# Head dimensions in neighbouring pairs, copies for q and k first, banks handed back early, and pauses in a planned Trainium2 kernel

## The chip, the cores and the metric

The kernel runs on one core of a Trainium2 chip. The metric is the device time of one execution in microseconds. Engines are called as in the profile: PE (TensorE), DVE (VectorE), ACT (ScalarE), POOL (GpSimd) and SP (SyncE, which issues the DMAs).

## The reference

One attention layer (A) and one gated layer (B) share their weights between two rounds, so that four layers follow each other over 2048 positions of 576 numbers in bf16:

```python
x = x + A(layernorm(x)); x = x + B(layernorm(x))
x = x + A(layernorm(x)); x = x + B(layernorm(x))

# A: 32 heads of 18 dimensions; position s sees s, s-2, ..., s-14
q, k, v = split(x @ wqkv)                     # wqkv [576, 3*576], columns (q|k|v, head, dim)
logits[h, s, w] = sum_d q[h, s, d] * k[h, s - 2w, d] * 18**-0.5     # w = 0..7, masked below 0
o[h, s, d] = sum_w softmax_w(logits)[h, s, w] * v[h, s - 2w, d]
A = o @ wo
# B: F = 4608
B = ((x @ w_gate) * (x @ w_up)) @ w_down
```

## The kernel before

The 2048 positions are cut into blocks of 256 (the first two, j=0 and j=1, have 128), and the two rounds of layers are interleaved: a block of round 1 runs when its inputs from round 0 are there, so 17 blocks j follow each other. For each block there is an attention part (layer norm, projection, logits, softmax, weighted sum, output product) and a gated part (gate and up products, h, down product). PE works on the gated part of one block while DVE and ACT work on the attention of the next.

**Order.** Nothing is left to a compiler's scheduler. Every operation is entered in a `Plan` with an engine, a cost in ns, a priority and a rank, and a list scheduler (`Plan.run`) walks through clocks that it keeps per engine and issues the instructions in the order that results. An operation with `alts` may go to either of two engines, by their clocks. A raw weight piece has a planned landing time (`late`). PSUM banks are handed out as slots: a *unit* is a pair of banks `pg`, `pu` (slots 0 to 2), and `acct`, `pa` are a fourth pair, which becomes a unit (slot 3) after the attention of block 2. While PE would wait in the first block, the plan puts dummy matmuls into `acct` (`fill`, L1212).

**First block ("boot").** x and wqkv come by DMA in raw form, five pieces of 128 rows (the last of 64) of the q and k columns (a) and of the v columns (b). The copies of `perm` (L391 to L421) put the columns in the order (dim, head): 128x512 for the first 16 dims of q or k, 128x256 halves for v (L408), and small tails for dims 16 and 17 (128x128, 128x64). The projection (L609) needs, per piece, the copies of that piece. Then follow the evictions of q and k (L727, L720, L691), the products q*k (L764), the sum over dims by a matmul with the 0/1 matrix `Esel` (L779), the softmax (max L805, difference L809, exp L817, sum L821, reciprocal L826, L829, L830), the spread of the softmax weights over the dims by `Bsel` (L845), its eviction to `ab` (L850, shown as L691 on DVE and L693 on ACT), the products with v (L878), their sums on PE (L882, L883), wo (L943), the residual (L913), layer norm (L474, L476, L492, L493, L497, L508), transposes (L527, L529), `xnT_B` (L534), and the first gate product (L996).

**Later blocks.** Logits come from L787, L768, L772 and L773 on DVE, the weighted sum from L878 and L900 on DVE. From block 3 on, the softmax weights go out to `a_dram` (L855) and come back four times (L858), spread over partitions. wo is L922. The gated part is L996, L1007 and L1020 on PE, `g_sb` on ACT (L1031), h on DVE (L1035, L1038) and the down products (L1052, L1089, L1090). `tok` (L553) is a copy of one element on ACT that keeps an order between PE and another engine.

The line of the plan that decides when an operation may start takes an operation of the same engine at its end:

```python
for p in o.deps:
    e = p.ready if p.eng != o.eng else p.end
```

Of the kernel before, what the change touches and what calls it, by code (L numbers as in the profile page):

```python
# [11 lines left out]
ALU = mybir.AluOpType  # L12
# [4 lines left out]
class Op:  # L17
    __slots__ = ("eng", "cost", "fn", "deps", "order", "succ", "n", "prio", "idx", "hold", "free",
                 "lat", "margin", "ready", "end", "nbytes", "use", "pair", "need", "rank", "late", "half", "res", "alts", "risk")
# [4 lines left out]
VP = ["ACT"] * 5  # L24
VT = ["ACT"] * 5
# [8 lines left out]
class Plan:  # L34
# [13 lines left out]
    def op(self, eng, cost, fn, r=(), w=(), prio=1, after=None, hold=None, free=None, margin=0, nbytes=0, use=None,  # L48
           pair=None, need=None, due=False, late=0, half=False, alts=None, risk=0):
# [59 lines left out]
    def run(self, slots):  # L109
# [10 lines left out]
        while cand:  # L120
            best = None
            urgent = {}
            for o in cand:
# [87 lines left out]
def kernel(  # L211
# [43 lines left out]
    a_dram = [dram.tile([P, 2 * CH], BF16, name=f"a_dram{i}") for i in range(2)]  # L255
# [12 lines left out]
    Bsel = sb("Bsel", [P, 4, 4, 32])  # L268
# [93 lines left out]
    def load_w(c):  # L362
        wr, c0, c1 = ((wrawa, 0, 2 * D), (wrawb, 2 * D, 3 * D))[c == "b"]
        for k in range(KT):
            for r_, rows in ((0, P),) if k < KF else ((0, TL), (TL, TL)):
                def fn(k=k, r_=r_, rows=rows):
# [6 lines left out]
                   nbytes=rows * (c1 - c0) * 2, prio=1 + (c == "b"), late=700 if c == "a" else 0)  # L373
# [4 lines left out]
    def setup_b():  # L378
# [11 lines left out]
        for k in range(KT):  # L390
            def perm(eng, cost, key, t3, rk, k=k):  # L391
                if t3 < 3:
                    wr = wrawb[:, k, :] if t3 == 2 else wrawa[:, k, t3 * D:(t3 + 1) * D]
                    src = wr.rearrange("p (h d) -> p d h", h=H)[:, 0:16, :]
                    dst = wqkv[:, k, t3 * 512:(t3 + 1) * 512].rearrange("p (d h) -> p d h", h=H)
                else:
                    t0, t1 = (0, 2) if t3 == 3 else (2, 3)
                    src = (wrawa, wrawb)[t3 - 3][:, k, :].rearrange("p (t h d) -> p t d h", t=t1 - t0, h=H)[:, :, 16:18, :]
                    dst = wqkv[:, k, 3 * 512:3 * D].rearrange("p (t d h) -> p t d h", t=3, h=H)[:, t0:t1]
                fn = {"DVE": nc.vector.tensor_copy, "POOL": nc.gpsimd.tensor_copy, "ACT": nc.scalar.copy}[eng]  # L400
                pl.rank = 0.5
                if t3 == 2:
                    for hf in range(2):
                        box = {}

                        def half(hf=hf, box=box):
                            f = {"DVE": nc.vector.tensor_copy, "ACT": nc.scalar.copy}[box["o"].eng]
                            f(dst[:, 8 * hf:8 * hf + 8], src[:, 8 * hf:8 * hf + 8])  # L408
                        box["o"] = op("ACT", 565, half, r=rk, w=[f"{key}{'ab'[hf]}"], prio=3, alts={"DVE": 320, "ACT": 565})
                else:  # L410
                    op(eng, cost, lambda: fn(dst, src), r=rk, w=[key], prio=2 + (t3 == 4))  # L411
                pl.rank = 0
            ra, rb = [[f"wraw{c}{k}"] if k < KF else [f"wrawt{c}0", f"wrawt{c}{TL}"] for c in "ab"]
            perm("DVE", 530, f"wq0_{k}", 0, ra)
            perm("DVE", 180, f"wq3_{k}", 3, ra)
            if k % 2:
                perm("DVE", 530, f"wq1_{k}", 1, ra)
            else:
                perm("ACT", 1000, f"wq1_{k}", 1, ra)
            perm(VP[k], {"ACT": 1050, "DVE": 560, "POOL": 1250}[VP[k]], f"wq2_{k}", 2, rb)  # L420
            perm(VT[k], {"ACT": 330, "DVE": 200, "POOL": 300}[VT[k]], f"wq4_{k}", 4, rb)  # L421

        def mk_sel():
            nc.gpsimd.memset(Esel[:], 0.0)
            nc.gpsimd.memset(Bsel[:], 0.0)
            for j in range(4):
                nc.gpsimd.affine_select(out=Esel[:], in_=Esel[:], compare_op=ALU.not_equal,
                                        fill=1.0, base=-32 * j, pattern=[[-1, 32]], channel_multiplier=1)
                nc.gpsimd.affine_select(out=Bsel[:, j], in_=Bsel[:, j], compare_op=ALU.not_equal, fill=1.0,
                                        base=-32 * j, pattern=[[0, 4], [-1, 32]], channel_multiplier=1)  # L430
# [817 lines left out]
```

## Time and profile before

| | us |
|---|---|
| median of 3 runs | 1043.29 (1042.44 to 1043.44) |
| the profiled execution | 1042.26 |
| its span | 1040.1 |
| PE busy | 1029.8 (17905 matmuls) |
| DVE busy | 775.8 |
| ACT busy | 437.1 |
| POOL busy | 8.9 |

The span is what the profile covers, from the first to the last instruction; the profiled execution was 2.2 us longer than it. Busy times of different engines overlap. A line such as `PE pu L609 <- DVE wqkv L411: 0.4, 1, 0.4` says that PE's instruction of line 609 waited for DVE's of line 411: 0.4 us in all, once, 0.4 us at most.

### The profile page before, as it was taken

The numbers are of one execution on the slowest core, as the hardware profiler recorded it, in microseconds if no ns is written. First come the engines' busy times: TensorE is split into PE (matmuls) and PEld (weight loads), VectorE is DVE, ScalarE is ACT, GpSimd is POOL, SyncE is SP. The second block draws the span as 40 slices with busy tenths as digits, with TensorE's granted clock in tenths as the row PEclk, the third lists the DMA queues.
The fourth block names the chain that finished last, engine by engine and source line by source line (L and its number), as shares of the span: only waits on it lengthen the run. The fifth ranks groups of instructions, "written<-read, shape, count | busy, mean of one in ns | idle before, by whom it ended". The sixth has DMA issues, their size and how long they took to land.

```text
span 1040.1 us, 40101 instructions
## 1 busy us (share of the span) xinstructions
PE 1029.8 (99%) x17905; PEld 810.1 (78%) x17905; DVE 775.8 (75%) x1450; ACT 437.1 (42%) x1169; POOL 8.9 (1%) x33
## 2 busy tenths in 40 slices
PE   7999999999999999999999999999999999999998
PEld 4788887778987787777777777877787778777776
DVE  8799696888768687877979697796977869574333
ACT  6744744354544653242344434334344433223231
POOL 3000000000000000000000000000000000000000
PEclk9999999999999999999999999999999999999999
DMA  9967424334543534443544426334442454343332
GB/s 275 338 201 213 107 83 130 120 97 104 116 138 88 103 108 111 129 107 95 151 131 106 108 74 161 96 83 109 121 115 94 103 127 114 101 154 84 124 97 70
DMA packets 144540, 129.66 MB, mean 125 GB/s; under 512 B 43440, under 2 KB 143728, under 8 KB 144368
## 3 DMA queue, kind: packets, MB, share of 16 engines
q1 hardware_dynamic: 144368, 127.10, 44.3%
q8 instruction: 140, 2.29, 0.9%
q14 instruction: 32, 0.26, 0.1%
HBM read 114.02 MB, written 4.19 MB: 114 GB/s over the span
## 4 chain that ended last, share of the span: by engine, by line
PE 94%; DVE 5%; ACT 1%; issue 1%; POOL 0%; POOLq 0%; DVEq 0%; ACTq 0%
PE pu L1020 19%; PE pg L1020 18%; PE pu L1089 8%; PE pa L1020 7%; PE pg L1089 6%; PE acct L1020 6%; PE pa L1089 4%; PE pg L609 4%; PE acct L1089 4%; PE pu L609 3%; PE pg L922 2%; PE pg L1090 1%; PE pu L996 1%; PE pg L996 1%; PE pu L1090 1%; PE acct L609 1%
## 5 line engine op out<-in xcount | busy, mean ns | idle before, releaser
L1020 PEld LDWEIGHTS <-wg 64*128 64x128 bf16 x4320 | 392.5, 94 | 35.2 <-issue 0.3
L1020 PE MATMUL pu<-xnT_B,wu 64*128 64x256 bf16 x3200 | 410.5, 269 | 0.1
L1020 PEld LDWEIGHTS <-wu 64*128 64x128 bf16 x4320 | 387.6, 94 | 28.1 <-ACT tok L553 0.2
L1020 PE MATMUL pg<-xnT_B,wg 64*128 64x256 bf16 x3200 | 409.4, 269 | 0.0
L1089 PEld LDWEIGHTS <-h 64*128 64x128 bf16 x2112 | 119.0, 94 | 107.0 <-issue 1.1
L1090 PE MATMUL pg<-wd,h 64*128 64x64 bf16 x960 | 181.4, 189 | 0.0
L1090 PE MATMUL pu<-wd,h 64*128 64x64 bf16 x960 | 181.4, 189 | 0.0
L1089 PE MATMUL pu<-wd,h 64*128 64x512 bf16 x672 | 173.8, 377 | 0.0
L1089 PE MATMUL pg<-wd,h 64*128 64x512 bf16 x672 | 173.7, 377 | 0.0
L1031 ACT CAST g_sb<-pg 128x512 bf16<-128x512 f32 x218 | 127.9, 588 | 93.6 <-PE pg L1020 80.4
L553 ACT COPY tok<-pu 1x1 f32<-1x1 f32 x287 | 42.2, 147 | 280.8 <-PE pu L1020 182.2
L1038 DVE TENSOR_TENSOR h<-pu,g_sb 128x512 bf16<-128x512 f32 x171 | 117.3, 690 | 56.9 <-ACT g_sb L1031 54.9
L1020 PE MATMUL pa<-xnT_B,wu 64*128 64x256 bf16 x1120 | 152.4, 269 | 0.0
L1020 PE MATMUL acct<-xnT_B,wg 64*128 64x256 bf16 x1120 | 152.4, 269 | 0.0
L1090 PEld LDWEIGHTS <-h 64*128 64x128 bf16 x2112 | 116.3, 95 | 0.7
L609 PEld LDWEIGHTS <-wqkv 64*128 64x128 bf16 (+1 forms) x2030 | 98.3, 94 | 16.3 <-issue 1.3
L1020 PE MATMUL pu<-xnT_B,wgu_t 64*128 64x256 bf16 x400 | 107.6, 269 | 0.0
L1020 PE MATMUL pg<-xnT_B,wgu_t 64*128 64x256 bf16 x400 | 107.6, 269 | 0.0
L1089 PE MATMUL pa<-wd,h 64*128 64x512 bf16 x384 | 99.3, 377 | 0.0
L1089 PE MATMUL acct<-wd,h 64*128 64x512 bf16 x384 | 99.2, 377 | 0.0
L609 PE MATMUL pg<-xnT_A,wqkv 64*128 64x256 bf16 (+2 forms) x809 | 94.9, 264 | 0.1
L609 PE MATMUL pu<-xnT_A,wqkv 64*128 64x256 bf16 (+1 forms) x789 | 93.4, 265 | 0.6 <-DVE wqkv L411 0.4
(189 smaller groups left out, 1573.0 us busy)
## 6 DMA issues: line engine op xcount, KB each, us to landing
wd<-in_B_w_down_dram SPq DMA_DIRECT2D x306, 288.0 KB, 4.3
scr<-a_dram SPq DMA_DIRECT2D x56, 128.0 KB, 2.6
wg<-in_B_w_gate_dram SPq DMA_DIRECT2D x6, 768.0 KB, 9.1
wu<-in_B_w_up_dram SPq DMA_DIRECT2D x6, 768.0 KB, 10.4
xb<-in_A_x_dram SPq DMA_DIRECT2D x7, 288.0 KB, 2.9
out_dram<-xf SPq DMA_DIRECT2D x14, 144.0 KB, 2.9
a_dram<-scr SPq DMA_DIRECT2D x14, 128.0 KB, 1.7
scr<-in_A_wqkv_dram SPq DMA_DIRECT2D x4, 288.0 KB, 4.2
```

Of the source, the lines that this page charges most:

```text
L553: box["at"] = nc.scalar.copy(tok[0:1, :], src())
L609: return nc.tensor.matmul(bank(p_, u)[0:m, e * n:(e + 1) * n], lhsT=wqkv[r_, k, w0:w0 + m], rhs=xnT_A[r_, k, c0:c0 + n], start=start, stop ...
L922: return nc.tensor.matmul(bank(hh, us[i])[:, 0:HD], lhsT=oT[rows, t, i * P:(i + 1) * P], rhs=wo_p[rows, t, hh * HD:(hh + 1) * HD], start=( ...
L996: nc.tensor.matmul(pt[:, e * n:(e + 1) * n], lhsT=w_[:, k, ft * P:(ft + 1) * P], rhs=xT[:, k, 0:n], start=(first and k == 0 and e == 0), s ...
L1020: return nc.tensor.matmul(ps[:, e * n:(e + 1) * n], lhsT=w_, rhs=xT[rows, k, 0:n], start=(first and e == 0 and k == 0), stop=(not first an ...
L1031: op("ACT", 490, lambda: nc.scalar.copy(g_sb[gs][:, 0:ul], pg[use["slot"]][:, 0:ul]), r=[f"wg_{j}_{u}"], w=[f"g{gs}"], prio=0, due=True)
L1038: op("DVE", 605, lambda: nc.vector.tensor_tensor(hb[hs][:, 0:ul], pu[use["slot"]][:, 0:ul], g_sb[gs][:, 0:ul], op=ALU.mult), r=[f"wu_{j}_{ ...
L1089: return [lambda: nc.tensor.matmul((pg, pu)[i][use["slot"]][:], lhsT=lhs, rhs=wt[rows, e % 2, 0:512], start=first, stop=fin, skip_group_ch ...
L1090: lambda: nc.tensor.matmul((pg, pu)[i][tl["slot"]][:, 0:TL], lhsT=lhs, rhs=wt[rows, e % 2, 512:D], start=first, stop=fin, skip_group_check ...
```

## The change

- The copies keep neighbouring dims of a head together: the order becomes (dim pair, head, dim in pair). `Esel`, `Bsel`, the rows of `wo_p` and the layout of `a_dram` follow. The planned costs of the copies change.
- The planned landing times of the raw pieces are a list, `LAND`, by piece.
- q and k copies get ranks 0 and 0.5, v copies 0.7. The k copies are on DVE, the last may go to ACT too; the v halves may go to either, the v tails go to ACT.
- The evictions to `ab` may go to DVE or ACT.
- `acct` and `pa` become a unit right after the spread of block 2, ahead of its output product and transposes.
- The plan adds `FLOW` = 110 ns where a DVE operation reads what another DVE operation wrote; some operations are exempt (`flow=False`). The step `l3` is entered as two operations.

Lines of the new file lie a little off: L609 becomes L607, L996 L1002, L1020 L1026, L1038 L1044, L913 L919, L922 L928 and L411 L410.

```diff
-VP = ["ACT"] * 5
-VT = ["ACT"] * 5
+LAND = (350, 750, 950, 1300, 1500, 1550)
+FLOW = 110
...
+        o.flow = {p for p in d if p.eng == eng == "DVE"} if flow else set()
...
                 for p in o.deps:
-                    e = p.ready if p.eng != o.eng else p.end
+                    e = p.ready if p.eng != o.eng else p.end + FLOW * (p in o.flow)
...
-    a_dram = [dram.tile([P, 2 * CH], BF16, name=f"a_dram{i}") for i in range(2)]
+    a_dram = [dram.tile([H, 4, 2 * CH], BF16, name=f"a_dram{i}") for i in range(2)]
...
-                   nbytes=rows * (c1 - c0) * 2, prio=1 + (c == "b"), late=700 if c == "a" else 0)
+                   nbytes=rows * (c1 - c0) * 2, prio=1 + (c == "b"), late=LAND[k + (r_ > 0)] if c == "a" else 0)
...
-                    src = wr.rearrange("p (h d) -> p d h", h=H)[:, 0:16, :]
-                    dst = wqkv[:, k, t3 * 512:(t3 + 1) * 512].rearrange("p (d h) -> p d h", h=H)
+                    src = wr.rearrange("p (h d e) -> p d h e", h=H, e=2)[:, 0:8]
+                    dst = wqkv[:, k, t3 * 512:(t3 + 1) * 512].rearrange("p (d h e) -> p d h e", h=H, e=2)
...
+                pl.rank = 0 if k + t3 == 0 else 0.5 if t3 in (0, 1, 3) else 0.7
...
-            perm("DVE", 530, f"wq0_{k}", 0, ra)
-            perm("DVE", 180, f"wq3_{k}", 3, ra)
-            if k % 2:
-                perm("DVE", 530, f"wq1_{k}", 1, ra)
-            else:
-                perm("ACT", 1000, f"wq1_{k}", 1, ra)
-            perm(VP[k], {"ACT": 1050, "DVE": 560, "POOL": 1250}[VP[k]], f"wq2_{k}", 2, rb)
-            perm(VT[k], {"ACT": 330, "DVE": 200, "POOL": 300}[VT[k]], f"wq4_{k}", 4, rb)
+            rb = rb + [f"wrawta{TL}"]
+            perm({"DVE": 390}, f"wq0_{k}", 0, ra)
+            perm({"DVE": 390, "ACT": 720} if k == KF else {"DVE": 390}, f"wq1_{k}", 1, ra)
+            perm({"DVE": 210}, f"wq3_{k}", 3, ra)
+            perm({"DVE": 250, "ACT": 360}, f"wq2_{k}", 2, rb)
+            perm({"ACT": 230}, f"wq4_{k}", 4, rb)
...
-                op("DVE", 276 + 2.02 * n, l3, r=pk, w=[sk], prio=prio)
+                op("DVE", 68 + 1.07 * n, l3, r=pk, w=[sk], prio=prio)
+                op("DVE", 68 + 1.07 * n, l4, r=[*pk, sk], w=[sk], prio=prio)
...
-                eng = fast and j0
-                op("DVE" if eng else "ACT", 600 if eng else 490,
+                box["o"] = op("ACT", 490, lambda j0=j0, b=b, box=box: cp(box["o"].eng == "DVE", late["ab"][:, j0:j0 + nb, 0:W * sq],
...
+                              r=[b.key, "ab"], w=[f"ab{j0 + e}" for e in range(nb)], prio=prio - 1, alts={"DVE": 600, "ACT": 490}, **b.drop())
+            if j == 2:
+                op("PE", 0, lambda: None, w=list(pool_keys["pa"]) + ["acct"], free="unit", use={"slot": NB})
+                pool["k"] = "unit"
...
-            op("SP", 600, lambda: nc.sync.dma_start(dr[:, 0:W * sq], late["a_c"][:, 0:W * sq]), r=["s13"], w=[f"adr{j % 2}"], prio=0,
+            op("SP", 600, lambda: nc.sync.dma_start(dr.rearrange("h j n -> j h n"), late["a_c"][:, 0:W * sq]), r=["s13"], w=[f"adr{j % 2}"], prio=0,
...
-                op("SP", 600, lambda g=g: nc.sync.dma_start(late["ab"][32 * g:32 * g + 32, :, 0:W * sq],
-                                                            dr[:, 0:W * sq].rearrange("(j h) n -> h j n", j=4)),
+                op("SP", 600, lambda g=g: nc.sync.dma_start(late["ab"][64 * (g // 2) + g % 2:64 * (g // 2) + 64:2], dr[:]),
...
-        if j == 2:
-            op("PE", 0, lambda: None, w=list(pool_keys["pa"]) + ["acct"], free="unit", use={"slot": NB})
```

Left out are the same step at the other places (`Esel`, `Bsel`, the loads of `wo_p`, the `perm` function's own body), `flow=False` on the residual sums in PSUM, a rank on the parts of the projection, and `oT` among the reads of L900.

More of the change, by code (lines that the diff above doesn't have):

```diff
@@ L18 @@
     __slots__ = ("eng", "cost", "fn", "deps", "order", "succ", "n", "prio", "idx", "hold", "free",
-                 "lat", "margin", "ready", "end", "nbytes", "use", "pair", "need", "rank", "late", "half", "res", "alts", "risk")
+                 "lat", "margin", "ready", "end", "nbytes", "use", "pair", "need", "rank", "late", "half", "res", "alts", "risk", "flow")
 POOLQ = False
 HOLD = 2
-VP = ["ACT"] * 5
-VT = ["ACT"] * 5
+LAND = (350, 750, 950, 1300, 1500, 1550)
+FLOW = 110
 SLACK = {"DVE": 500, "ACT": 300, "PE": 0, "POOL": 0, "SP": 0}
@@ L48, in op @@
     def op(self, eng, cost, fn, r=(), w=(), prio=1, after=None, hold=None, free=None, margin=0, nbytes=0, use=None,
-           pair=None, need=None, due=False, late=0, half=False, alts=None, risk=0):
+           pair=None, need=None, due=False, late=0, half=False, alts=None, risk=0, flow=True):
         o = Op()
@@ L267 @@
     Esel = sb("Esel", [P, 32])
-    Bsel = sb("Bsel", [P, 4, 4, 32])
+    Bsel = sb("Bsel", [P, 4, 2, 32, 2])
     cap = sb("cap", [P, W, HALO])
@@ L396, in perm @@
                 else:
                     t0, t1 = (0, 2) if t3 == 3 else (2, 3)
[L398 to L409, printed above, removed]
-                else:
-                    op(eng, cost, lambda: fn(dst, src), r=rk, w=[key], prio=2 + (t3 == 4))
+                    src = (wrawa, wrawb)[t3 - 3][:, k, :].rearrange("p (t h d) -> p t h d", t=t1 - t0, h=H)[:, :, :, 16:18]
@@ new lines, in perm, with fn @@
+                    dst = wqkv[:, k, 3 * 512:3 * D].rearrange("p (t h e) -> p t h e", t=3, h=H)[:, t0:t1]
+                pl.rank = 0 if k + t3 == 0 else 0.5 if t3 in (0, 1, 3) else 0.7
+                for hf in range(2 if t3 == 2 else 1):
+                    box = {}
+                    def fn(hf=hf, box=box):
+                        f = {"DVE": nc.vector.tensor_copy, "ACT": nc.scalar.copy}[box["o"].eng]
+                        if t3 == 2:
+                            f(dst[:, 4 * hf:4 * hf + 4], src[:, 4 * hf:4 * hf + 4])
+                        else:
+                            f(dst, src)
+                    box["o"] = op("DVE", 0, fn, r=rk, w=[f"{key}{'ab'[hf]}" if t3 == 2 else key], prio=2 + (t3 == 4), alts=alts)
@@ L772, in l3, with l4 @@
                 nc.vector.tensor_tensor(s1[:, :, 0:n], prod[:, :, 0, 0:n], prod[:, :, 2, 0:n], op=ALU.add)
+            def l4(p_=p_):
+                prod, s1 = late["prod"][p_ % 2], late["s1"][p_]
                 nc.vector.tensor_tensor(s1[:, :, 0:n], s1[:, :, 0:n], prod[:, :, 4, 0:n], op=ALU.add)
```

31 lines of the change are left out of this document (16 added, 15 removed).

## The prediction

> **What bounds the kernel now.** I read the page's table of engines and its 40 slices first, then the list of what PE waited for, then PE's busy time by stretches, then the chain of waits over the first 31 us.
>
> ```profile
> PE 1029.8 (99%) x17905; PEld 810.1 (78%) x17905; DVE 775.8 (75%) x1450; ACT 437.1 (42%) x1169; POOL 8.9 (1%) x33
> ...
> PEclk9999999999999999999999999999999999999999
> ```
>
> PE is busy for 1029.8 of 1040.1 us and the granted clock is 1.00 in every stretch below, so only 10.3 us are not matmul time. The change leaves the real matmuls alone (17905 against 17904, one dummy fill less), so it can move only those 10.3 us and the switches between matmuls of different height.
>
> ```profile
> PE pg L527 <- ACT xn L503: 1.3, 1, 1.3
> PE acct L1212 <- DVE g_sb L1216: 1.2, 1, 1.2
> PE pu L779 <- DVE scr L764: 1.2, 2, 0.8
> PE pa L1090 <- DVE h L1038: 0.8, 1, 0.8
> PE pu L882 <- DVE scr L878: 0.7, 1, 0.7
> PE pg L996 <- ACT xnT_B L534: 0.6, 1, 0.6
> PE pg L845 <- ACT scr L817: 0.4, 1, 0.4
> PE pu L609 <- DVE wqkv L411: 0.4, 1, 0.4
> PE pu L609 <- ACT tok L553: 0.3, 1, 0.3
> ```
>
> ```profile
> 0.00:10.00 10.00, 7.12 (x54) 3.74 (x54) 6.53 (x17) 6.24 (x9) 8.92 (x33) 1.00 0.77 229
> 10.00:20.00 10.00, 7.67 (x137) 4.38 (x135) 9.59 (x24) 8.35 (x22) 0.00 (x0) 1.00 0.99 282
> ...
> 45.00:100.00 55.00, 54.93 (x851) 46.69 (x850) 49.80 (x97) 28.17 (x65) 0.00 (x0) 1.00 0.76 223
> 380.00:400.00 20.00, 19.19 (x334) 14.74 (x332) 19.27 (x39) 9.06 (x28) 0.00 (x0) 1.00 0.23 52
> ```
>
> (Per stretch: busy time of PE, PEld, DVE, ACT, POOL, then clock.) All but two of the waits lie before 30 us. Busy PE in the boot flatters, because fills (L1212) run wherever it would sit idle: what counts there is when the first GLU matmul (L996) starts, 29.764 us. After it I find five stalls by the matmuls' starts: 0.42 at 42.5 (the fence copy `tok` L553 queued on ACT behind two L503 of 0.87), 0.13 at 96.8, 0.12 at 120.3, 0.26 at 260.4 (DVE xf L913) and 0.98 at 389.2 (DVE h L1038): 1.9 us in all. The boot's chain:
>
> ```profile
> 4.93 4.28 DVE wqkv L411 x10
> ...
> 12.13 0.88 DVE scr L764 x2
> ...
> 15.16 0.60 DVE wqkv L408 x2
> 15.79 0.44 DVE mx L805
> ...
> 17.92 0.36 DVE zs L826
> 18.31 0.19 DVE rz L829
> ...
> 27.91 0.66 ACT xn L508
> ```
>
> **1. Copies by pairs, q and k first (path).** DVE's copies run back to back from 4.854 to 10.391. Spacing of a 128x512 is 0.529 alone and on average 0.645 (five of them, 0.556 to 0.815) while POOL works until 9.05; a 128x128 takes 0.18. No row shows the pair pattern. Upper bound: no gain, 0.529. Lower bound: the contiguous bf16 128x512 product h L1035, 0.336 from start to start. I take 0.40, nearer the contiguous row, as every destination and each pair of the source is contiguous. DVE now does two 512 copies and a tail for each of the first four weight pieces, the first ahead of nmr L497, from the landing at 4.567: per piece (2 x 0.40 + 0.18) x 1.22 (0.645/0.529) = 1.20, so 4.70 + 4 x 1.20 = 9.50, and q and tail of the fifth (last landing 9.166) end at 10.08 instead of 10.39. ACT makes the fifth k copy from 9.2; even at its old 1.02 it ends at 10.2 instead of 10.36. The two L408 halves that still stand before k's eviction L691 shrink from 0.30 to about 0.23 each. L764 thus starts 0.40 earlier. Bounds: with 0.336 the last landing rules and it is about 0.8; with 0.529 the piece costs 1.51, q and tail end at 11.45, and it is 1.0 us later.
>
> [...]
>
> **2. After the logits (path).** The two L408 copies between the last L764 and mx L805 leave DVE. What is next late is PE's L779, whose last matmul ends at 15.54: mx starts at about 15.59 instead of 15.79, -0.20. In the softmax, a copy (L691) and mv now stand between dependent instructions. A dependent neighbour starts 0.034 after its forerunner where an independent one overlaps by 0.08, so each pause is 0.11; two go: -0.23. Sum at the first L878: -0.83.
>
> **3. Second rstd on ACT (path).** Behind rstd1 (ends 27.682) ACT now has L492 and L493 of the next block (0.29 + 0.20 = 0.50) before xn L508, which until now waited 0.23 for nmr: +0.27. First GLU matmul: -0.55, at about 29.2.
>
> **4. Four ab copies (L691) from ACT to DVE in j=1 and j=2.** 4 x 0.61 = 2.4 us more of DVE. In j=1 DVE sat idle 2.2 us (45.93 to 48.13) for just this copy, so the chain of L878 starts earlier instead. In j=2 I followed DVE's new order by the row's spacings to the last L773: about 69.2, where PE reaches L779 at about 69.6. Cost nil, but the cover is only 0.4 us.
>
> **5. Pauses in the plan.** Two chains interleaved remove some 0.11 us per pair. Between 365.65 and 389.5 DVE made about ten such pauses (1.1 us) and then came 0.98 us late with h L1038; zs, L826 and L824 also move ahead of an h product there, so the write to `a_dram` goes out sooner. I count this stall as gone (-0.98). At 42.5 both L503 now stand before the fences: -0.42. The three small ones are half kept: -0.25. Sum -1.65.
>
> **6. Banks earlier, other order on PE.** acct and pa join the units sooner, which saves waits that j=2 does not show (54.93 busy in 55.00): nil. The new order switches between 128-row and 64-row matmuls six times more after the first L996 (64 for 58); a switch costs 0.09 to 0.12 in the starts: +0.57. New stalls of the new order cannot be read from this trace; bounds 0 to 2, the measure being the old order's 1.9 in five places. As its pauses are planned, I take +0.4.
>
> **7. `a_dram` and SP.** The write becomes scattered rows of 1 KB and each of four reads 32 rows of 4 KB instead of 128 of 1 KB: read 2.6 us to landing now. Neighbouring rows: xb, 288 KB in rows of 1152 B, 2.9; wd, 288 KB, 4.3. Nil taken, -1 to +2 us per landing as bounds. SP issues the same 503 instructions; the earlier q projection near 357 (L609, 4.3 us up) needs its second transpose, which landed at 355.67 and is issued ahead of more wd loads now. wo L922 is later by some 40 matmul groups, with over 14 us to the first use of xnT_B. Selects, wo rows, LAND: nil.
>
> Sum: -0.55 - 1.65 + 0.57 + 0.40 = -1.23 from the profiled 1042.26 (span 1040.1 and 2.2 around it) = 1041.0. The median of the runs lies 1.03 above the profiled run, so about 1042.1; since the cautious +0.4 is the softest term, I forecast 1041.8. A measurement of this kernel can tell about 0.2%, 2.1 us, from no change, so this is inside that.
>
> **Rivals.**
>
> A. *The boot gains 0.8 and no new stall appears.* -0.55 becomes -0.95, all of the 1.9 goes, +0.57: -2.3; with dependent pauses also gone in blocks whose DVE lag now hides under switches, -3. Median 1040.3 to 1041. For: few, known stalls, all named by the plan's new costs. Against: six more switches, cover of 0.4 in j=2. Chance 0.33.
>
> B. *Pairs copy no faster.* Boot +1.0 - 0.43 + 0.27 = +0.84 instead of -0.55: sum +0.2, 1043.4. For: no row of this trace has such a pattern. Against: the contiguous row at 0.336. Chance 0.10. It covers also the case that the change does not do what its name says.
>
> C. *The 4 KB reads land late (slower).* DVE's first L878 waits for `a_dram` in the queue, and h L1038 of the GLU stands behind it. It waited so 20.9 us in ten places, once 5.57, and that block later stalled PE for 0.98. If 32 long rows landed 2.6 us later (2.6 becomes 5.2), fourteen blocks would wait as long as that one or half as long; at 0.3 to 0.4 each, +4 to +5.5 against the sum, 1045 to 1047. It decides from some 2 us of delay. Against: longer rows carry more bytes per us here (xb 99 KB per us against 49). Chance 0.08.
>
> D. *A new wait on PE in the new order*, likeliest at L609 near 353 us: if the second xnT_A transpose lands as late as 355.67 less the 1.5 us saved before it, while PE is there at 352, PE stands about 2.2 us; with one like it in a sister block, +3 net, 1045 to 1046. Against: SP's earlier issue. Chance 0.12.
>
> E. *Faster copies shut POOL out.* Beside POOL's selects the copies of before are already spaced 0.645 instead of 0.529, and selects (L429) take up to 0.70 instead of 0.35. If the new copies stopped POOL altogether, its 4.2 us of selects (4.88 to 9.05) would run from 10.1 to 14.3. The last L779 starts at about 14.8 in the new boot and needs them, so +0 to +0.5, inside the forecast. Chance 0.03. [...]
>
> **How the numbers follow.** Forecast 0.34 as it stands (1041.2 to 1043.0). Faster by over 0.2% means under 1041.2: A and the better edge of the forecast, 0.38. Slower by over 0.2% means over 1045.4 or nearly all of C and most of D: 0.17. The rest 0.45. The range takes in A (1039.6) and the lower half of D (1045.0), and leaves out C and the worst of D.
>
> **What would show it.** Right: 128x512 L411 spaced near 0.40; first L764 near 11.7, first L878 near 18.6, first GLU matmul near 29.2; ACT with L493 before L508; no wait on `tok` near 42 and none on h near 389; PE busy about 1029 to 1030. Wrong: spacing still 0.53; PE waiting at L779 of j=2, at L609 near 352 or at L922; DVE's wait for `a_dram` above 25 us; the first GLU matmul after 29.8.

## The result, and the profile after

The changed kernel takes 1045.14 us (median of 9 runs, 1044.06 to 1047.85), the kernel before on the same chip 1042.49 (9 runs, 1041.95 to 1043.44). The ratio is 1.0025 [1.0017, 1.0033]: slower by 2.65 us, with an interval that lies wholly above 1. The forecast was 1041.8, and the median lies just beyond the end of its range, 1045.0.

The profiled execution took 1046.15, with a span of 1044.0. From the profile page after, the engines' busy time and the chain that ended last:

```profile
PE 1031.7 (99%) x17904; PEld 824.2 (79%) x17904; DVE 756.6 (72%) x1454; ACT 430.2 (41%) x1165; POOL 9.4 (1%) x33
...
PE 88%; DMA 6%; DVE 3%; SPq 2%; ACT 1%; issue 0%; DVEq 0%
```

DVE has 19 us less to do, yet the end comes 3.9 us later, and DMA, which had no share in the chain of before (PE 94%, DVE 5%), now has 6%. What PE waited for (us in all, times, the longest):

```profile
PE pg L525 <- ACT xn L501: 1.9, 1, 1.9
PE pu L782 <- DVE scr L764: 1.8, 4, 0.6
PE acct L1216 <- DVE g_sb L1220: 1.2, 1, 1.2
PE pa L1026 <- DVE xf L1075: 0.7, 2, 0.5
PE pg L1002 <- ACT xnT_B L532: 0.6, 1, 0.6
PE pg L1026 <- DVE xf L1075: 0.5, 1, 0.5
PE pg L1058 <- DMA wd<-in_B_w_down_dram: 0.5, 1, 0.5
PE pu L607 <- DVE xf L1075: 0.5, 1, 0.5
PE pu L1026 <- DVE xf L1075: 0.5, 1, 0.5
```

L1075 is new in this list: the additions of the down products to the residual, which hand a block's PSUM banks back. The matmuls that waited for them start at 141.6, 187.5, 425.6, 426.4 and 799.8. The stalls that the prediction had named are gone (`tok` at 42.5, h at 389.2); the stretches show it (PE, PEld, DVE, ACT, POOL busy, then clock, DMA share and GB/s):

```profile
0.00:10.00 10.00, 6.65 (x36) 3.66 (x37) 5.95 (x18) 4.08 (x7) 9.12 (x29) 0.89 0.68 197
10.00:20.00 10.00, 8.23 (x151) 5.66 (x149) 8.60 (x23) 6.63 (x23) 0.25 (x7) 0.94 0.96 249
45.00:100.00 55.00, 55.00 (x851) 47.17 (x848) 48.69 (x98) 26.86 (x61) 0.00 (x0) 1.00 0.82 232
380.00:400.00 20.00, 20.00 (x349) 18.72 (x347) 19.47 (x39) 9.75 (x30) 0.00 (x0) 1.00 0.26 54
410.00:430.00 20.00, 19.01 (x335) 14.84 (x332) 11.68 (x19) 4.93 (x14) 0.00 (x0) 1.00 0.42 124
```

So the 3.9 us of the span are 1.07 in the boot (first gate product L1002 at 30.83 instead of 29.76) and 2.85 behind it (1010.04 against 1007.19 from there to PE's last matmul). Of the 2.85, 2.05 are stalls (3.93 against 1.88, by the matmuls' starts). About 0.57 go to the six more switches, counted again here (64 against 58) and priced as in the prediction; 0.2 is not accounted for. Of the 3.93, some 3 are the five waits for L1075, and 0.6 is one at 40 us for a weight load (L1058).

The chain of waits at 410 to 426, where two of the five stalls lie, tells where they come from:

```profile
412.73 0.61 DVE scr L828
413.33 0.02 issue
413.35 3.32 DMA a_dram<-scr
416.67 0.02 issue
...
417.92 0.58 SPq L865
418.50 0.04 issue
418.55 4.02 DMA scr<-a_dram
...
422.69 0.83 DVE oT L884
423.52 1.47 DVE scr L884 x2
424.99 1.34 DVE xf L1075 x3
```

The softmax weights leave DVE at 413.3; the write to `a_dram` is 3.3 us under way, SP issues the four reads after it, and DVE has them at 422.6, having stood 6 us. Behind the three products L884 that then run, the additions L1075 are queued, though the last down product into their banks had ended at 418.2. The trace of PE's instructions shows who waits for those:

```profile
425.64 0.27 PE L1026 MATMUL pg<-xnT_B,wg 64*128 64x256 bf16 x1 [0.53 <-DVE xf L1075]
426.37 0.27 PE L1026 MATMUL pu<-xnT_B,wu 64*128 64x256 bf16 x1 [0.46 <-DVE xf L1075]
```

### The profile page after: what moved, and what is told of

The parts are those of the page before. It is cut to its first block, busy times and chain, and to the rows that moved or that the text cites. A ratio compares the mean times of both kernels' runs of the same rounds, so it can differ in the third digit from the quotient of the medians.

```text
span 1044.0 us, 40093 instructions
## 1 busy us (share of the span) xinstructions
PE 1031.7 (99%) x17904; PEld 824.2 (79%) x17904; DVE 756.6 (72%) x1454; ACT 430.2 (41%) x1165; POOL 9.4 (1%) x33
## 4 chain that ended last, share of the span: by engine, by line
PE 88%; DMA 6%; DVE 3%; SPq 2%; ACT 1%; issue 0%; DVEq 0%
PE pu L1026 19%; PE pg L1026 18%; PE pa L1095 7%; PE acct L1095 5%; PE pa L1026 5%; PE pu L1095 5%; PE acct L1026 5%; PE pg L607 4%; PE pu L607 4%; PE pg L1095 3%; PE pg L928 2%; DMA scr<-a_dram 1%; DMA a_dram<-scr 1%; DMA wd<-in_B_w_down_dram 1%; PE pu L1002 1%; PE pg L1002 1%
## 5 line engine op out<-in xcount | busy, mean ns | idle before, releaser
L1026 PE MATMUL pu<-xnT_B,wu 64*128 64x256 bf16 x3440 | 441.1, 269 | 0.5 <-DVE xf L1075 0.5
L1026 PE MATMUL pg<-xnT_B,wg 64*128 64x256 bf16 x3440 | 440.0, 269 | 0.5 <-DVE xf L1075 0.5
L1026 PEld LDWEIGHTS <-wg 64*128 64x128 bf16 x4320 | 393.3, 94 | 33.7 <-issue 2.1
L1026 PEld LDWEIGHTS <-wu 64*128 64x128 bf16 x4320 | 389.7, 94 | 27.2 <-issue 0.9
L1044 DVE TENSOR_TENSOR h<-pu,g_sb 128x512 bf16<-128x512 f32 x181 | 123.5, 688 | 87.4 <-ACT g_sb L1037 85.4
L1095 PE MATMUL pa<-wd,h 64*128 64x512 bf16 x648 | 165.9, 377 | 0.0
L1095 PE MATMUL acct<-wd,h 64*128 64x512 bf16 x648 | 165.9, 377 | 0.0
L1096 PE MATMUL pg<-wd,h 64*128 64x64 bf16 x864 | 163.3, 189 | 0.0
L1096 PE MATMUL pu<-wd,h 64*128 64x64 bf16 x864 | 163.3, 189 | 0.0
L1026 PE MATMUL pa<-xnT_B,wu 64*128 64x256 bf16 x880 | 119.8, 269 | 0.7 <-DVE xf L1075 0.7
L1026 PE MATMUL acct<-xnT_B,wg 64*128 64x256 bf16 x880 | 120.2, 269 | 0.0
L1026 PE MATMUL pu<-xnT_B,wgu_t 64*128 64x256 bf16 x430 | 115.7, 269 | 0.0
L1026 PE MATMUL pg<-xnT_B,wgu_t 64*128 64x256 bf16 x430 | 115.7, 269 | 0.0
L607 PEld LDWEIGHTS <-wqkv 64*128 64x128 bf16 (+1 forms) x2030 | 102.6, 95 | 13.0 <-issue 2.3
L1095 PE MATMUL pu<-wd,h 64*128 64x512 bf16 x408 | 104.6, 377 | 0.0
L1095 PE MATMUL pg<-wd,h 64*128 64x512 bf16 x408 | 104.4, 377 | 0.0
L607 PE MATMUL pg<-xnT_A,wqkv 64*128 64x256 bf16 (+2 forms) x881 | 103.0, 266 | 0.2 <-ACT xnT_A L537 0.2
L607 PE MATMUL pu<-xnT_A,wqkv 64*128 64x256 bf16 (+1 forms) x861 | 101.1, 267 | 0.5 <-DVE xf L1075 0.5
```

The costliest lines, as they stand in the source:

```text
L607: return nc.tensor.matmul(bank(p_, u)[0:m, e * n:(e + 1) * n], lhsT=wqkv[r_, k, w0:w0 + m], rhs=xnT_A[r_, k, c0:c0 + n], start=start, stop ...
L1026: return nc.tensor.matmul(ps[:, e * n:(e + 1) * n], lhsT=w_, rhs=xT[rows, k, 0:n], start=(first and e == 0 and k == 0), stop=(not first an ...
L1044: op("DVE", 605, lambda: nc.vector.tensor_tensor(hb[hs][:, 0:ul], pu[use["slot"]][:, 0:ul], g_sb[gs][:, 0:ul], op=ALU.mult), r=[f"wu_{j}_{ ...
L1095: return [lambda: nc.tensor.matmul((pg, pu)[i][use["slot"]][:], lhsT=lhs, rhs=wt[rows, e % 2, 0:512], start=first, stop=fin, skip_group_ch ...
L1096: lambda: nc.tensor.matmul((pg, pu)[i][tl["slot"]][:, 0:TL], lhsT=lhs, rhs=wt[rows, e % 2, 512:D], start=first, stop=fin, skip_group_check ...
```

## The experiments

Ratios are to the kernel before, measured on the same chip; its medians there were 1042.58 to 1042.96. "Way" is the time from the end of the softmax product (L828, L824 in the old file) to the first product with v (L884, L878 in the old file), the median over the blocks in which DVE stood waiting. "Rest" is the time from the first gate product to PE's last matmul in the profiled execution. The diffs are shortened: the `op(...)` calls around the shown expressions are left out.

**The old round trip in the changed kernel** (`x1_adram_old`).

```diff
-    a_dram = [dram.tile([H, 4, 2 * CH], BF16, name=f"a_dram{i}") for i in range(2)]
+    a_dram = [dram.tile([P, 2 * CH], BF16, name=f"a_dram{i}") for i in range(2)]
-    nc.sync.dma_start(dr.rearrange("h j n -> j h n"), late["a_c"][:, 0:W * sq])
+    nc.sync.dma_start(dr[:, 0:W * sq], late["a_c"][:, 0:W * sq])
-    nc.sync.dma_start(late["ab"][64 * (g // 2) + g % 2:64 * (g // 2) + 64:2], dr[:])
+    nc.sync.dma_start(late["ab"][64 * (g // 2) + g % 2:64 * (g // 2) + 64:2, :, 0:W * sq],
+                      dr[:, 0:W * sq].rearrange("(j h) n -> h j n", j=4))
```

> The changed kernel with the round trip over a_dram in its old form: one row of 1 KB per partition written in a row, and reads of 32 x 4 rows of 1 KB (into every second partition). Nothing else differs. In the trace of the changed kernel the write is issued in 0.59 us (0.34 before), the first read follows it after 3.4 us (1.75), the reads are issued 0.63 apart (0.47), and from the end of L828 to the first L884 it takes 8.1 to 9.6 us against 5.7 to 6.6 in the undisturbed blocks before. Theory T1 (the new form of the round trip is late, DVE's queue waits behind it, and the banks that DVE empties come free too late): the way from L828 to L884 falls to about 6.2 us, the waits of PE for DVE xf L1075 (2.4 us) go, and the time is 2 to 2.5 us less than the changed kernel's, 1042.6 to 1043.1. Rival T2 (the five waits for L1075 come from the new order of DVE, whatever the reads do): the way gets shorter and the waits stay, at most 0.5 us won.

Measured 1041.59 (1041.36 to 1041.93), ratio 0.9991 [0.9982, 1.0]: 3.55 us under the changed kernel, more than the 2 to 2.5 expected, though the way fell only to 7.76 and not to 6.2. All waits for L1075 are gone from PE's list, of which this is the one line behind 30 us:

```profile
PE pg L1058 <- DMA wd<-in_B_w_down_dram: 0.4, 1, 0.4
```

The rest is 1006.51, 3.5 less than after and 0.7 less than before. T1 holds for the waits: the loss is `a_dram`, and the boot is not needed to explain it.

**The new form of `a_dram` alone in the kernel before** (`x4_before_newform`): the write as in the change, and reads of whole rows, still into neighbouring partitions.

```diff
-    nc.sync.dma_start(late["ab"][32 * g:32 * g + 32, :, 0:W * sq], dr[:, 0:W * sq].rearrange("(j h) n -> h j n", j=4))
+    nc.sync.dma_start(late["ab"][32 * g:32 * g + 32], dr[:])
```

> The kernel before with nothing but the new form of the round trip (a_dram as heads x 4 x 512 numbers, written scattered, read back as 32 rows of 4 KB). Theory T1: from the end of L824 to the first L878 it takes 2 to 3 us more in each of the 14 blocks, and PE, which before waited only once behind a late block (0.98 at 389), waits in several: 1.5 to 4 us slower than before. Rival T2: the order of the kernel before has the cover, and it is within 0.5 us of it.

Measured 1044.25 (1043.39 to 1044.80), ratio 1.0014 [1.0005, 1.0023]: +1.67. The rest grows by 1.36 (1008.55 against 1007.19), the way from 6.40 to 7.89, 1.5 where 2 to 3 were expected, and the same kind of wait appears in the old order, L1069 being the line of these additions there:

```profile
PE pu L1020 <- DVE xf L1069: 0.8, 2, 0.5
```

**Reads of 1 KB rows again** (`x2_adram_pad`). The changed kernel with 64 unused columns in `a_dram`, so that a read can't run over row ends.

```diff
-    a_dram = [dram.tile([H, 4, 2 * CH], BF16, name=f"a_dram{i}") for i in range(2)]
+    a_dram = [dram.tile([H, 4, 2 * CH + 64], BF16, name=f"a_dram{i}") for i in range(2)]
```

> The changed kernel with its a_dram tile padded by 64 columns, so that the write still scatters rows of 1 KB and the reads cannot be joined into rows of 4 KB: they are 32 x 4 rows of 1 KB, not next to each other. It tells the two halves of the round trip apart. If the long read rows are what is late, the reads are issued 0.47 apart again and land some 2.5 us after their issue, and about 1.2 of the 2.5 us per block comes back; if it is the scattered write, the 3.4 us from the write to the first read stay and the way from L828 to L884 stays above 7.5 us. I expect both to have a share: 7 to 7.5 us, and a time 0.5 to 1.5 us under the changed kernel's.

Measured 1046.68 (1045.07 to 1047.84), ratio 1.0035 [1.0023, 1.0048], and a way of 8.95 against 9.03: nothing is won back. The length of the rows read is not the cause, and the part of my expectation that hung on it fell. What is left are the write and the partitions that the reads go to.

**Old rows, 4 KB apart in memory** (`x14_rows_apart`, x1 with one more edit; the reads follow the rows). If the write is slow because its rows are scattered, this one, with 128 rows of 1 KB just as scattered, is slow too; if it is slow because the outermost dimension of its pattern has only 4 steps (4 x 32 x 512), this one, with 128 steps, is not.

```diff
-    a_dram = [dram.tile([P, 2 * CH], BF16, name=f"a_dram{i}") for i in range(2)]
+    a_dram = [dram.tile([P, 4, 2 * CH], BF16, name=f"a_dram{i}") for i in range(2)]
-    nc.sync.dma_start(dr[:, 0:W * sq], late["a_c"][:, 0:W * sq])
+    nc.sync.dma_start(dr[:, 0, 0:W * sq], late["a_c"][:, 0:W * sq])
```

> The changed kernel with the old round trip, but the rows that the write puts into a_dram lie 4 KB apart instead of 1 KB (each of 128 partitions writes 1 KB, the reads follow). It tells two causes of the late write apart. In the changed kernel the window around one write to a_dram shows 132 packets, 4 of them under 512 B, and the DMA engines a quarter busy; before it shows 144, 16 of them small, and the engines 0.7 to 0.9 busy. Theory T9 (the new write's pattern has 4 as its slowest dimension and so runs on 4 of the 16 DMA engines): here the slowest dimension is 128, the write shows 16 small packets, the first read follows 1.8 us after the write's issue, and the time is within 0.4 us of 1041.59. Rival T10 (rows scattered over DRAM are late whatever the engines): the first read follows after 3 us or more and the time is 1044 to 1045.

Measured 1041.88 (1041.13 to 1043.19), ratio 0.9992 [0.9982, 1.0001], and from the start of the write's issue to the first read 1.95 us (before 1.77, after 3.37). The DMA view of one write shows the difference. Its first line is the mean busy share of the 16 DMA engines in 40 slices of the window, in tenths. After, 359.6 to 363.1 us:

```profile
DMA  0000000000000001313212292222222223100000
DMA packets 133, 0.15 MB, mean 42 GB/s; under 512 B 4, under 2 KB 132, under 8 KB 132
```

With rows apart, 357.0 to 359.0 us:

```profile
DMA  0000000000000000001599999872100000000090
DMA packets 145, 0.15 MB, mean 74 GB/s; under 512 B 16, under 2 KB 144, under 8 KB 144
```

The 128 packets of 1 KB are the same. After, 0.1 to 0.3 of the engines are busy over 1.7 us (one slice shows 0.9), and 4 small packets close the transfer; with 128 steps 0.5 to 0.9 of them are busy in eight of the eleven slices of some 0.5 us, and there are 16 small packets. This is how 4 engines against 16 would look; the view doesn't name the engines, so that the number of steps sets the number of engines is my guess and not shown. The 128 steps also take one dimension out of the write's pattern (128 x 512 for 4 x 32 x 512), which no run tells apart from the number of steps.

The round trip in the kernels that tell its forms apart, medians in us (x11, described below, is the kernel before with the pair layout and the old write):

| kernel | way | write's issue | write to first read | spacing of reads | rows read, partitions |
|---|---|---|---|---|---|
| before | 6.40 | 0.34 | 1.77 | 0.47 | 1 KB, neighbouring |
| x4 | 7.89 | 0.56 | 3.30 | 0.46 | 4 KB, neighbouring |
| x11 | 7.10 | 0.34 | 1.78 | 0.64 | 1 KB, every second |
| x1 | 7.76 | 0.34 | 1.78 | 0.65 | 1 KB, every second |
| x14 | 7.58 | 0.34 | 1.95 | 0.65 | 1 KB, every second |
| after | 9.03 | 0.59 | 3.37 | 0.63 | 4 KB, every second |
| x2 | 8.95 | 0.58 | 3.49 | 0.64 | 1 KB, every second |

("Write to first read" begins where SP begins the write's issue.) The 2.6 us of after are thus two prices: 1.5 to 1.6 for the new write, and 0.7 to 1.4 for reads into every second partition. The lowest figure for these is the cleanest: x11 issues the same instructions in the same order as before, and DVE waited in ten blocks of each. For x1 and x14 the way is the median of only four and five blocks. Three times 0.16 to 0.18 of it is SP's issue; the rest would be a later landing. The second price comes with the pair layout. x1 keeps it without one stall for L1075, and in the old order of x11 it brings one wait of 0.3 for these additions; in the changed order it is the write that stalls PE.

**The layer norm's small step ahead of the first copy** (`x3_nmr_first`, and with the old round trip `x5_old_and_nmr`). In the changed order `nmr` L495 (minus mean times rstd) stands behind the first copy; it began at 5.46 in the profile after (4.78 before), because the first copy had waited for its piece until 5.03.

```diff
-LAND = (350, 750, 950, 1300, 1500, 1550)
+LAND = (1000, 1000, 950, 1300, 1500, 1550)
```

> The changed kernel with the first two planned landings at 1000 ns instead of 350 and 750. The only difference in the order of instructions is on DVE: nmr L495 stands ahead of the first weight copy L410 again, as before the change. In the changed kernel nmr stood behind that copy, whose piece landed late (the copy began at 5.03), nmr ended at 5.61 instead of 4.94, and PE sat idle from 4.66 to 6.57; then the granted clock fell to 0.50 for 3 us. Theory T3 (nmr behind the copy costs the boot, and the longer idle time lets the clock fall): nmr ends near 4.95, the clock stays 1.00 in every microsecond of the boot, the first L1002 starts 0.9 to 1.6 us earlier than 30.84, near 29.5, and the time is 0.7 to 1.5 us less, 1043.6 to 1044.4. Rival T4 (the clock falls for another reason, such as fewer dummy matmuls later or an uneven state of the chip): the clock still falls to 0.50 in some runs and the gain is 0.3 to 0.5 us.

> The changed kernel with the old round trip over a_dram and nmr L495 ahead of the first weight copy (planned landings 1000, 1000). Against the run with the old round trip alone (1041.59 us) only the place of nmr differs, and DVE's order there by one instruction. Theory T3 (nmr behind a copy that waits for a landing makes the boot later where the piece lands late): the spread of the runs narrows at the upper end and the median is 0.2 to 0.6 us lower, 1041.0 to 1041.4. Rival T4 (the first piece usually lands at 4.1 to 4.6, as in three of the five profiles so far, and nmr at 4.84 costs nothing): within 0.15 us of 1041.59.

x3: 1044.56 (1042.67 to 1045.02), ratio 1.0013 [1.0004, 1.0022], 0.6 under the changed kernel. x5: 1041.52 (1040.66 to 1042.58), ratio 0.9991 [0.9983, 1.0], no different from x1. So the gain of the step's place is 0.6 in one pair and 0.1 in the other, and the intervals tell neither from nothing; the first lies below T3's 0.7 to 1.5. The core's mean clock is under 1.00 in 6 of the 11 runs of each, as against 4 of 9 of the changed kernel, so this step is not what lets the clock fall, and T3 doesn't hold. Both profiles have their first gate product at 29.17, the forecast's 29.2. The two differ from each other in the round trip alone: 3.0 us in the median and 2.6 in the rest (1008.75 against 1006.12), a second price for it beside x1's.

**Each kernel once more** (`x12_before_again`, `x13_after_again`).

> The kernel before, unchanged, for a second profile of its boot: how far the first gate product L996 (29.76 in the first profile, 30.66 in the variant of it that touches only a_dram) moves with the landings. I expect 29.5 to 30.7, and 1007.2 us from there to PE's last matmul.

> The changed kernel, unchanged, for a second profile: the waits for L1075 after 130 us and the 3.4 us from the write to a_dram to its first read must be there again, 1009 to 1010 us from the first L1002 to PE's last matmul against 1007.2 before. Whether nmr is late and the clock falls in the boot is open; where the first piece lands by 4.6, the first L1002 starts at 29.2 to 30.0.

Before: 1042.33, first gate product at 29.77, rest 1007.16. After: 1044.64, 30.18 and 1009.18. This second pair differs by 0.4 in the boot and 2.0 behind it, and the same five places wait for L1075 (140.4 to 798.3). The waits come back, the boot's 1.07 doesn't. Its first copy began at 4.45, so 29.2 to 30.0 was expected and 30.18 is a miss. What seems to keep this boot from 29.17 is PE itself. The projection's matmuls in 7.6 to 10.3 us, grouped by shape (busy us, mean ns of one), first in this run, then in x5:

```profile
L607 PE MATMUL pu<-xnT_A,wqkv 128*128 128x128 bf16 x14 | 2.1, 311 | 0.0
L607 PE MATMUL pg<-xnT_A,wqkv 128*128 128x128 bf16 x12 | 1.9, 312 | 0.0
```

```profile
L607 PE MATMUL pu<-xnT_A,wqkv 128*128 128x128 bf16 x20 | 2.0, 221 | 0.2 <-DVE wqkv L410 0.2
L607 PE MATMUL pg<-xnT_A,wqkv 128*128 128x128 bf16 x13 | 1.4, 220 | 0.0
```

The slow ones start 0.107 apart instead of 0.056. The profile after has 30 of them, and there the granted clock is 0.50 in 8 to 11 us; in this run 24 lie at a granted clock of 1.00. For 24 of them that is 1.2 us, and L764 starts 1.03 later than in x5 (12.57 against 11.54). Matmuls at this spacing are in 9 of 12 profiles with the changed boot order and in 2 of 4 with the old one. Where they are, the first gate product came 0.8 to 1.7 us later than x5's 29.17 (29.98 in x1, 30.68 in x15, 30.83 after, where the first piece was late too) and 0.9 later in x4 than before (30.66 against 29.76).

**More dummy matmuls in the boot** (`x8_fill`: x5 with 40 fills for 24), to keep PE from this state.

```diff
-                    n = int((t - max(real, 900) - 150) * 0.75 / each)
+                    n = int((t - max(real, 900) - 150) * 1.1 / each)
```

> The kernel with the old round trip and nmr first, and about 16 more dummy matmuls in the boot (1.1 instead of 0.75 of each planned idle time). In the changed kernel the granted clock fell to 0.50 for about 3 us in the boot in 4 of 9 runs (mean clock 0.998), in 16 of 27 of the three variants with its boot, in 5 of 38 with the boot of before. Theory T7 (too little matmul work between 11 and 16 us lets the clock fall): with more of it no run shows 0.998, and the runs' upper end comes down by up to 1 us; median 0 to 0.5 lower unless the fills stand in the way of real matmuls. Rival T8 (the fall has nothing to do with how busy PE is): 0.998 in half of the runs as before, and a time equal or up to 1 us longer for the fills in the way.

Measured 1042.32 (1041.41 to 1046.78), ratio 1.0001 [0.9992, 1.0011]: no gain over x5. The core's mean clock was under 1.00 in only one of 11 runs, against 6 of 11 in x5, so this half of T7 holds and T8 doesn't, and the profile has no stretch of slow matmuls. But its boot, 29.68, is longer than x5's. The profile lost 2.5 us at 372 to 375 to one round trip that took 10.8, its first read 3.8 after the write's issue, and PE waited for L1075: the same path from a late round trip to PE, with the old form. So the runs can't price the clock by itself.

**The copies alone** (`x11_pairs_only`): the kernel before with the pair layout, every order as it was, the old write; the reads go into every second partition. The other places of the layout, as in the change, are left out here.

```diff
-                    src = wr.rearrange("p (h d) -> p d h", h=H)[:, 0:16, :]
-                    dst = wqkv[:, k, t3 * 512:(t3 + 1) * 512].rearrange("p (d h) -> p d h", h=H)
+                    src = wr.rearrange("p (h d e) -> p d h e", h=H, e=2)[:, 0:8]
+                    dst = wqkv[:, k, t3 * 512:(t3 + 1) * 512].rearrange("p (d h e) -> p d h e", h=H, e=2)
```

> The kernel before with the layout by pairs alone (copies, Esel, Bsel, rows of wo, reads of ab into every second partition); every engine runs the same instructions in the same order, and the write to a_dram is the old one. It prices the copies by themselves. From the trace of the changed kernel a 128x512 copy by pairs is spaced 0.30 alone on DVE (0.529 before) and ACT's takes 0.65 (1.11). Forecast's step 1 with that price: DVE's copies end with the last landing, near 9.9 instead of 10.39, L764 starts 0.3 to 0.5 earlier, and the two L408 copies ahead of mx take 0.2 less: 0.5 to 0.8 us less than before, 1041.8 to 1042.2. Against it stand reads of ab spaced 0.65 instead of 0.47 (0.5 us more per block), which may give back up to 0.5 at the late block near 389. Rival: the boot waits for landings and the copies are worth nothing, within 0.15 us of before.

Measured 1042.24 (1041.14 to 1042.96), ratio 0.9993 [0.9985, 1.0002]: −0.72, inside what was expected though not told from nothing by its interval. Its one profile is of its longest run (1042.96), with slow matmuls in the boot and L764 at 12.68, so the steps of the boot can't be read from it.

**The plan's pauses, the banks, the ab copies**, each undone in x1.

```diff
-FLOW = 110
+FLOW = 0
```

> The changed kernel with the old round trip and FLOW = 0, so that the plan knows no pause between dependent DVE operations (the whole order after the boot is planned anew). It prices the step that the forecast put at -1.65 for the stalls. Theory T5 (the planned pauses took the old stalls away): stalls of the old kind come back on PE after 30 us, 1 to 2 us in all instead of 0.59, and the time is 1 to 2 us more than 1041.59. Rival T6 (the old stalls went by the luck of another order): any order is as good, within 0.5 us of 1041.59, and the stalls after 30 us are below 0.8.

1042.38 (1041.71 to 1043.49), ratio 0.9999 [0.999, 1.0008]: 0.8 more than x1, or 0.6 when each is taken against the kernel before on its own chip. That is less than T5's 1 to 2 and more than T6's 0.5, and the intervals of x7 and x1 overlap: neither is shown. The rest is 0.5 longer (1007.03), and stalls of 0.6 at 117 (`tok`) and 0.3 at 859 are back.

```diff
-            if j == 2:
-                op("PE", 0, lambda: None, w=list(pool_keys["pa"]) + ["acct"], free="unit", use={"slot": NB})
-                pool["k"] = "unit"
...
         pl.rank = 60
...
+        if j == 2:
+            op("PE", 0, lambda: None, w=list(pool_keys["pa"]) + ["acct"], free="unit", use={"slot": NB})
```

> The changed kernel with the old round trip, and acct and pa handed to the units after the whole attention of block 2, as before the change. The forecast priced the early hand-over at nil. Theory: within 0.5 us of 1041.59 (a new order has its own small stalls). Rival: the early banks carry the gain, and without them the time is 1 us or more above 1041.59.

1041.93 (1040.77 to 1042.89), ratio 0.9994 [0.9986, 1.0003]: 0.3 more than x1 (0.2 against each one's own kernel before), with one stall of 0.77 at 115.5 (`tok`), while the rest is no longer (1006.41).

```diff
-      alts={"DVE": 600, "ACT": 490}
+      alts={"DVE": 600} if fast and j0 else {"ACT": 490}
```

> The changed kernel with the old round trip and the ab evictions of j=1 and j=2 held on ACT as before the change (the first block's second one stays on DVE). The forecast priced their move to DVE at nil. Theory: within 0.5 us of 1041.59. Rival: DVE's idle time at 46 to 48 was worth something, and without the move j=1's chain is later and PE waits for it: 0.5 to 1.5 us more than 1041.59.

1041.28 (1040.34 to 1045.86), ratio 0.9988 [0.9979, 0.9996]: 0.3 less than x1 (0.7 against each one's own kernel before), the lowest median of all. It is the one kernel here whose interval lies wholly under 1.

**The last with nmr first as well** (`x15_best`).

> A version put together from what the runs showed: the changed kernel with the old round trip, the ab evictions of j=1 and j=2 on ACT, and nmr ahead of the first copy. Expected 1041.0 to 1041.4, 1.3 to 1.7 us under before. If the place of nmr is worth nothing, it equals the run with the evictions on ACT (1041.28).

1042.10 (1041.12 to 1043.88), ratio 0.9994 [0.9985, 1.0003], not the 1041.0 to 1041.4 expected. The rest is as good as ever (1006.25), but the profiled boot ended at 30.68, with 12 slow matmuls at 15 to 16 us. The kernels with the old round trip, from 1041.3 to 1042.1, can't be ranked among each other by these medians.

## Why the prediction was wrong, point by point

**The step that failed is 7, `a_dram` and SP: "Nil taken, -1 to +2 us per landing as bounds".** I compared the rows' lengths and took bounds per landing from loads with long rows; neither the write's form (3.37 us to the first read instead of 1.77) nor the partitions that the reads go to (0.63 to 0.65 us of issue each instead of 0.46 to 0.47), the two things that cost time, stand in it. The write's delay, 1.6, lay inside those bounds; what I didn't carry was from the delay to the end. In x1, with a way of 7.8, no wait for L1075 is left; with 9.0 the delay passes on to what DVE has queued behind L884, five times 0.4 to 0.7 us of stall in four blocks. It depends on the block: single blocks in x10 and x14 took 8.9 and 9.2 without such a wait. Measured: −0.99 us in the median against before without the new form (x1) and +2.65 with it, so the term is about +3.6 in the changed order, or +3.0 by x3 against x5. In the old order it is +1.67 (x4), with 1.5 us of delay. That I took nil in the sum while my own upper bound stood at the threshold of rival C, "some 2 us of delay", is where the forecast could have been saved.

**Rival C** (chance 0.08) had the place and the threshold: 2.6 us more on the round trip, and PE stalled. It had the wrong half, since the reads' rows are innocent (x2, a way of 8.95 against 9.03), and the wrong waiter: PE shows no wait for the h product L1044, while it waited for the bank-freeing additions. Its price, 4 to 5.5, was above the 3.0 to 3.6 measured, as four blocks stalled PE and not fourteen. Its sign, DVE's wait for `a_dram` above 25 us, was wrong as well; the sign that did come, a first gate product after 29.8 (30.83 and 30.18), belongs to the boot, where most of the loss does not lie. DVE waited thus in all (us, times, longest), before, after, in x1 and in x11:

```profile
DVE oT L878 <- DMA scr<-a_dram: 20.9, 10, 5.6
```

```profile
DVE oT L884 <- DMA scr<-a_dram: 18.6, 9, 6.0
```

```profile
DVE oT L884 <- DMA scr<-a_dram: 8.8, 4, 4.7
```

```profile
DVE oT L878 <- DMA scr<-a_dram: 28.4, 10, 6.0
```

Against before the sum has even shrunk, because the new plan waits less whatever the round trip: with x1's own form of it, the old order of x11 waits 28.4. Against x1, the same plan, the sum after has doubled. A wait must be compared in the same order.

**1, copies.** Forecast 0.40 for a 128x512. The groups by shape in 0 to 12 us, after and then before:

```profile
L410 DVE COPY wqkv<-scr 128x512 bf16<-128x512 bf16 x9 | 3.6, 432 | 1.4 <-DMA scr<-in_A_wqkv_dram 1.4
L410 DVE COPY wqkv<-scr 128x128 bf16<-128x128 bf16 x5 | 2.5, 508 | 0.0
L410 ACT COPY wqkv<-scr 128x512 bf16<-128x512 bf16 x1 | 0.7, 650 | 1.6 <-DMA scr<-in_A_wqkv_dram 1.6
```

```profile
L411 DVE COPY wqkv<-scr 128x512 bf16<-128x512 bf16 x7 | 4.7, 690 | 0.0
L411 DVE COPY wqkv<-scr 128x128 bf16<-128x128 bf16 x5 | 1.6, 315 | 0.0
L411 ACT COPY wqkv<-scr 128x512 bf16<-128x512 bf16 x3 | 3.3, 1114 | 0.8 <-DMA scr<-in_A_wqkv_dram 0.8
```

At the shortest they start 0.29 to 0.30 apart (before 0.529), under my lower bound of 0.336, and the nine of after span 0.29 to 0.53. But the tails of 128x128 beside POOL's selects take 508 ns on average instead of 315 and give a part back. With the projection's matmuls 0.056 apart (x5), L764 starts 0.59 earlier; forecast 0.40. Rival B falls.

**2 and 3.** In x5, mx gains 0.17 more (forecast 0.20) and the first L884 0.32 more (0.23). Then 0.41 is lost between it and the first residual L919, which I had carried through as nothing: DVE's L911 stands 0.3 and PE's L949 0.4 for it. The rstd pair on ACT costs 0.09, not 0.27. The boot's sum is −0.59 against the forecast −0.55, right by two errors that cancel. The profile after, at 30.83, shows none of it: there the first piece landed late (the first copy began at 5.03) and 30 matmuls were 0.107 apart, a term that the forecast put at nothing.

**4.** "Cost nil": 0.3 to 0.7 worse (x1 against x10), with intervals that overlap.

**5 and 6.** x1's rest is 0.68 less than before: stalls 0.59 instead of 1.88 and +0.57 of switches. The forecast was −1.65 + 0.40 + 0.57 = −0.68. The old stalls went, as said. That the sums agree is partly luck: what is left in x1 is mostly one new stall for a weight load at 39 us (L1058, 0.4 in the list above), which my guess of 0.40 met and which is 0.1 in x5. Without FLOW the rest is 0.5 longer (x7); the early banks show nothing in the rest (x9), and neither price is told from nothing by the medians.

**Rivals A, D, E.** Stalls did go as A said, but the new round trip made others. The wait of D at L607 near 353 didn't come; the one at L607 in the list above is for L1075. POOL ended its selects at 9.6 (9.05 before) and nothing waited for them, so E fell.

Steps 1 to 6 give −1.23 in the forecast; x1, which is the change without the new form of the round trip, gives −0.99 (its interval touches no change), and x5 −1.2. In x1 the agreement is loose: its profiled boot is 0.22 longer than before and its rest 0.68 shorter. The base of 1043.29 was itself high, a median of three runs; nine runs gave 1042.49.

**Open:** why PE falls to half rate (0.107 instead of 0.056 between matmuls) in some boots and not in others. The changed order shows it more often (9 of 12 against 2 of 4), which is too few to call the order its cause. With more fills (x8) the core's mean clock was 1.00 in 10 of 11 runs, and the time was no shorter (1042.32 against 1041.52 in x5).

## What to carry to other kernels

When a DMA's pattern changes, look at its outermost dimension before its rows: here a write with 4 steps outermost kept 0.1 to 0.3 of the DMA engines busy and had the first read behind it at 3.37 us, one with 128 steps 0.5 to 0.9 and 1.95 (x14), with the same 128 packets of 1 KB. A delay on a round trip is to be followed to everything queued on the waiting engine behind the wait, small instructions that only hand a buffer back included. And one profile of a boot is not the boot: two profiles of the changed kernel put its first gate product 0.65 us apart.

## What the runs showed of the hardware that was not expected

- A write of 128 KB with 4 steps outermost took 3.37 us from the start of its issue to the first read behind it, 0.59 of it the issue itself (after, medians); with 128 steps 1.77 and 0.34 (before; in x14, whose rows are scattered too, 1.95 and 0.34).
- SP took 0.63 to 0.65 us per read of 128 KB into every second partition (rows of 4 KB in after; of 1 KB in x1, x2, x11 and x14) and 0.46 to 0.47 into neighbouring ones (4 KB in x4, 1 KB before).
- Copies of 128x512 by neighbouring pairs started 0.29 to 0.30 us apart on DVE at the shortest and took 650 ns on ACT (after), against 0.529 us and 1114 ns for single elements (before). Tails of 128x128 beside POOL's selects were 0.38 to 0.56 us apart (after), against 0.20 to 0.30 (before).
- In the second profile of the changed kernel (x13) 24 projection matmuls started 0.107 us apart instead of 0.056 while the granted clock was 1.00.
